# Routing blocks and logits of the first expert layer: table entry moved to the next list, logits in column fourths, unread products at the head

## The chip, the core and the metric

The kernel runs on one core of one Trainium2 chip, as one program with one launch. The metric is the device time of the execution in microseconds (us), as the median of three runs; the profile is one further execution.

## The reference

Attention over 2 batches, 8 heads, 576 positions of 64 numbers, with a mask of blocks of 64 positions, gives 1152 rows of 512. A first expert layer sends each row to one of 8 experts, at most 288 rows to each; a second sends each row to two of 8 experts, by noisy logits.

```python
attn_out = _attn_ref(q, k, v)                      # softmax(q k^T / 8, block mask) v
x = attn_out.transpose(0, 2, 1, 3).reshape(1152, 512)
# first layer: e = argmax(x @ w_gate); kept if fewer than 288 rows came to e before
out[i] = gate_w[i] * (relu(x[i] @ w1[e]) @ w2[e])
# second layer
noisy = x @ w_gate + log1p(exp(x @ w_noise)) * noise
top2 = the two largest of noisy; top2_w = softmax of the two
out[i] = sum over the two e of top2_w * (relu(x[i] @ w1[e]) @ w2[e])
```

## The kernel before

The program has three stages. Attention works through 8 pairs of heads. A planner in the kernel (`Weave`) sets the order of the instructions on every engine when the program is built.

In the first expert layer each expert has a list of instructions, which another planner, `Flow`, puts in order from estimated costs and from a row of numbers in `PAR` (weights on the rest of the path by engine, a seed, due times). For every expert the program holds a small list (up to 128 rows: `one_block`) and a large one (`blocks`, 288 rows); a branch on the number of rows picks one. If an expert has more than 256 rows, a further short list for the last 32 follows the large one. In this execution experts 0 to 4 take the small list, 5, 6 and 7 the large one, and 6 the further one. Below, "list 2" is the list of expert 2. The large weights come from DRAM in units of 512 KB, and ACT and DVE split every unit into a high and a low part (L167, L170) one expert ahead; every product is three passes on TensorE (PE), of high and low parts (L198 to L200), apart from one unit of each expert that is used whole in f32 (L184).

In each list of an expert beside its own products stand three more jobs:

- `splits`: the weights of the next expert.
- `row1` (L1441) and `prep` (L1015 to L1021): POOL gathers the rows of the next expert from the DRAM table `x_d` into `xr` by an indirect DMA; PE transposes them, and ACT and DVE make the high part `xh` and the low part `xl`.
- `post`: the routing of a finished block of 128 rows for the second layer. PE transposes the block (L1243) and ACT copies it (L1247). PE makes the 16 logits of the second layer's gate and noise (`logit`, L1252, four accumulating f32 matmuls that record as eight). A chain of small operations on ACT and DVE (L1256 to L1281) finds the two experts of each row, as a one-hot `M`. PE ranks the rows within their experts (`rank`, L1286 and L1288) and POOL counts them into `cum` (`count`, L1292). DVE works out the two destinations (L1315 to L1325). `slots`, `cells` and `filled` (L1329 to L1340, DVE) spread them into two factors S and C, PE multiplies these (`table`, L1345), and DVE adds the product to the table `T2` (L1349), which tells the second layer which row and weight stands in which place of which expert. On POOL `place` (L1228 to L1233) prepares the row's index and `send` (L1236) scatters the block to `x_d`.

A small list holds one `post` (of the block of the expert before), a large list two (that, and its own first block), the further list one (expert 6's second block), and the first list of the second layer (`KNOWN`) one: 12 in this execution. List 0 has none. In list 7 the rows of the first block of the second layer are already gathered from `x_d` (`rows2`, L1418).

All engines take their instructions in the order of the lists, so a PE instruction that waits holds back all behind it.

Of the kernel before, what the change touches and what calls it, by code (L numbers as in the profile page):

```python
# [12 lines left out]
I32 = mybir.dt.int32  # L13
# [16 lines left out]
PAR = [dict(P=0.05, A=0.2, V=0.3, G=0.2, fit=0.52, late=0.548, dma=2.7, when=5.0, split=0, prep=1.8, post=1.85, last=2.5, seed=8387, noise=0.2),  # L30
       dict(P=0.2, A=0.2, V=0.2, G=0.1, fit=0, late=0.32, dma=2.44, when=10.0, split=6.3, prep=0, post=0.3, last=8.0, seed=5942, noise=0.2),
# [15 lines left out]
def attention_moe_moe2(ctx, tc, q, k, v, wg1, w1a, w2a, cap, wg2, wn2, noise, w1b, w2b, out):  # L47
# [45 lines left out]
    wcat = consts.tile([128, KD, 16], F32, name="wcat")  # L93
# [203 lines left out]
    with ExitStack() as actx:  # L297
# [628 lines left out]

    nc.vector.tensor_scalar(cum, ioe, float(NG), None, op0=OP.mult)
# [5 lines left out]
    class Flow:  # L933
# [4 lines left out]
        def __init__(self, kind=OTHER):  # L938
            self.kind, self.par, self.table = kind, PAR[kind], None
# [279 lines left out]
    def post(F, pd, n=128, deps=(), ranks=None, last=False, early=()):  # L1219
# [5 lines left out]
        def place():  # L1225
            fl = tl["fl"] = small.tile([128, 3], F32, name="fl")
            v = tl["v"] = small.tile([128, 2, 2], F32, name="v")
# [90 lines left out]
        def dest():  # L1318
            d = tl["di"] = small.tile([128, 3, 2], I32, name="di")
# [7 lines left out]
        def slots():  # L1327
            S2 = tl["S2"] = small.tile([128, 2, 128], F32, name="S2", bufs=1)
            nc.vector.tensor_tensor(S2[:n], tl["di"][:n, 1, :, None].to_broadcast([n, 2, 128]),  # L1329
                                    fslot[:n, None, :].to_broadcast([n, 2, 128]), op=OP.is_equal)  # L1330

        def cells():
            g = [n, 2, 8 * NG]
            C1 = tl["C1"] = small.tile([128, 2, 8 * NG], F32, name="C1", bufs=1)
            nc.vector.tensor_tensor(C1[:n], tl["di"][:n, 2, :, None].to_broadcast(g), iog[:n, None, :].to_broadcast(g), op=OP.is_equal)

        def filled():
            g = [n, 2, 2, 8 * NG]
            C2 = tl["C2"] = small.tile([128, 2, 2, 8 * NG], F32, name="C2", bufs=1)
            nc.vector.tensor_tensor(C2[:n], tl["C1"][:n, :, None, :].to_broadcast(g), tl["v"][:n, :, :, None].to_broadcast(g), op=OP.mult)  # L1340

        def table(bank):
            tl["T"] = bank[:, 0:16 * NG]
            for j in range(2):
                nc.tensor.matmul(tl["T"], tl["S2"][:n, j], tl["C2"][:n, j].rearrange("p a g -> p (a g)"), start=(j == 0), stop=(j == 1))  # L1345

        def enter():
            c = T2[:, :, :, 0:NG]
            nc.vector.tensor_tensor(c, tl["T"].rearrange("p (a e g) -> p a e g", a=2, e=8), c, op=OP.add)  # L1349
# [5 lines left out]
        lg = F.add("P", 0.85, logit, [a], take="sm")  # L1355
# [456 lines left out]
```

## Time and profile before

| | before |
|---|---|
| median of 3 runs | 547.79 us (546.66 to 547.98) |
| the profiled execution | 548.82 us, of which the span of the profile 547.2 us |
| PE busy | 514.5 us, 94% |
| DVE, ACT, POOL busy | 69%, 54%, 26% |
| DMA | 99.17 MB, mean 181 GB/s |

The profiled execution is 1.03 us above the median, and its own time 1.62 us above its span. Attention fills the first 138 us or so, the first expert layer goes to about 345 us, the second layer from there to the end. A row of the timeline gives the start and the duration of the instructions merged into it, and in brackets how long the engine had been idle before, and what ended that.

### The profile page before, as it was taken

What the parts mean: (1) busy time and instruction counts of PE and PEld (TensorE: products, weight loads), DVE (VectorE), ACT (ScalarE), POOL (GpSimd) and SP (SyncE); (2) the same over time, 40 slices, a digit from 0 to 9 for tenths busy, and PEclk for the clock granted to TensorE, in tenths of its full rate; (3) what the DMA queues carried; (4) which work ended last, traced back from release to release, by engine and by line L of the source; (5) the groups of instructions that cost most, each with busy time, mean ns of one, the idle gap of its engine ahead of it and who ended that gap; (6) DMA issues with size and microseconds to landing.
All of it is one profiled execution on the core that took longest, in us unless ns stands there. A gap on an engine that the chain in (4) does not pass through costs nothing. (4 is left out here: it accounts for less than half of the span.)

```text
span 547.2 us, 10101 instructions
## 1 busy us (share of the span) xinstructions
PE 514.5 (94%) x3381; PEld 421.4 (77%) x3381; DVE 379.1 (69%) x1008; ACT 294.1 (54%) x580; POOL 143.1 (26%) x225
## 2 busy tenths in 40 slices
PE   3999999999978999999999998999999999999996
PEld 2777777877755876796975976888889797789794
DVE  6889988898748887867575567647657492658441
ACT  5888878882355776653544346335536171726130
POOL 3000000000355344313423224114415051455031
PEclk9999999999999999999999999999999999999999
DMA  6988987501667788754642444528585674285120
GB/s 136 217 196 244 243 224 177 173 2 65 225 213 267 241 264 280 269 181 133 208 123 77 133 151 141 182 90 282 208 299 192 225 264 175 79 311 190 66 67 35
DMA packets 71176, 99.17 MB, mean 181 GB/s; under 512 B 37130, under 2 KB 40586, under 8 KB 71088
## 3 DMA queue, kind: packets, MB, share of 16 engines
q1 hardware_dynamic: 63600, 83.16, 48.4%
q0 software_dynamic: 6432, 14.71, 8.7%
q8 instruction: 39, 0.64, 0.5%
q14 instruction: 49, 0.40, 0.3%
q10 hardware_dynamic: 1056, 0.26, 0.2%
HBM read 87.53 MB, written 12.25 MB: 182 GB/s over the span
## 5 line engine op out<-in xcount | busy, mean ns | idle before, releaser
L170 DVE TENSOR_TENSOR wl<-raw,wh 128x512 fp32r<-128x512 f32 x140 | 91.5, 684 | 12.9 <-ACT wh L167 12.6
L167 ACT ACTIVATE wh<-raw 128x1024 fp32r<-128x1024 f32 x70 | 71.2, 1052 | 20.6 <-PEq L1776 12.5
L170 DVE TENSOR_TENSOR both<-raw,both 128x512 fp32r<-128x512 f32 x100 | 66.0, 684 | 9.0 <-ACT both L167 8.5
L167 ACT ACTIVATE both<-raw 128x1024 fp32r<-128x1024 f32 x50 | 51.4, 1054 | 10.0 <-PEq L1776 8.3
L198 PE MATMUL h<-xh,wh 128*128 128x256 f32 (+1 forms) x184 | 52.8, 287 | 0.5
L199 PE MATMUL h<-xl,wh 128*128 128x256 f32 (+1 forms) x184 | 52.6, 286 | 0.0
L200 PE MATMUL h<-xh,wl 128*128 128x256 f32 (+1 forms) x184 | 52.5, 285 | 0.0
L1018 ACT ACTIVATE xh<-tp 128x512 fp32r<-128x512 f32 (+1 forms) x37 | 18.9, 536 | 56.3 <-PE tp L1015 54.6
L1583 POOL DMA_INDIRECT out_dram<-o,T2i x16 | 18.6, 1164 | 99.7 <-DVE o L1580 97.6
L1021 DVE TENSOR_TENSOR xl<-tp,xh 128x512 fp32r<-128x512 f32 (+1 forms) x37 | 21.8, 609 | 31.1 <-ACT xh L1018 30.9
L1145 ACT ACTIVATE hh<-h 128x512 fp32r<-128x512 f32 (+1 forms) x46 | 24.1, 523 | 34.7 <-PE h L200 29.8
L198 PE MATMUL h<-xh,both 128*128 128x256 f32 (+1 forms) x136 | 39.1, 288 | 2.7 <-DVE hl L1148 1.4
L1148 DVE SCALAR_TENSOR_TENSOR hl<-h,hh 128x512 fp32r<-128x512 f32 (+1 forms) x46 | 27.4, 596 | 18.0 <-ACT hh L1145 16.9
L199 PE MATMUL h<-xl,both 128*128 128x256 f32 (+1 forms) x136 | 39.0, 287 | 0.0
L200 PE MATMUL h<-xh,both 128*128 128x256 f32 (+1 forms) x136 | 38.8, 285 | 0.0
L198 PE MATMUL y<-wh,hh 128*128 128x512 f32 (+1 forms) x94 | 38.3, 408 | 0.0
L200 PE MATMUL y<-wh,hl 128*128 128x512 f32 (+1 forms) x94 | 37.0, 394 | 0.0
L199 PE MATMUL y<-wl,hh 128*128 128x512 f32 (+1 forms) x94 | 37.0, 394 | 0.0
L526 PE MATMUL s<-both 128*128 128x256 f32 (+2 forms) x128 | 33.0, 370 | 4.2 <-ACT both L468 2.5
L550 ACT ACTIVATE pt<-s,negmax 128x128 f32<-128x128 f32 (+3 forms) x64 | 33.4, 526 | 6.3 <-DVE negmax L537 5.1
L198 PEld LDWEIGHTS h<-xh,wh 128*128 128x128 f32 x184 | 34.7, 189 | 1.9 <-issue 1.6
L1437 POOL MEMSET xr<- 128x524 f32 x3 | 1.5, 547 | 132.2 <-DVE T1f L811 132.2
(295 smaller groups left out, 1331.1 us busy)
## 6 DMA issues: line engine op xcount, KB each, us to landing
raw<-in_moe_w_dram SPq DMA_DIRECT2D x120, 512.0 KB, 5.5
wf<-in_moe_w_dram SPq DMA_DIRECT2D x8, 512.0 KB, 4.3
out_dram<-zero SPq DMA_DIRECT2D x3, 768.0 KB, 5.7
both<-both SPq DMA_DIRECT2D x14, 160.0 KB, 2.7
raw<-in_q_dram SPq DMA_DIRECT2D x16, 128.0 KB, 4.3
vn<-in_v_dram SPq DMA_DIRECT2D x16, 128.0 KB, 2.6
both<-both SPq DMA_DIRECT2D x14, 144.0 KB, 2.6
raw<-in_k_dram SPq DMA_DIRECT2D x14, 128.0 KB, 4.6
```

Of the source, the lines that this page charges most:

```text
L167: nc.scalar.activation(h, t, AF.Copy)
L170: (nc.gpsimd if part == 3 else nc.vector).tensor_sub(l[:, c], t[:, c], h[:, c].bitcast(F32))
L198: nc.tensor.matmul(o, sh, mh, start=first, stop=False)
L199: nc.tensor.matmul(o, sh, ml, start=False, stop=False)
L200: nc.tensor.matmul(o, sl, mh, start=False, stop=last)
L526: nc.tensor.matmul(o, w[:, i, h, 128 * t:128 * t + 128], w[:, i + 2, h, 64 * h:64 * h + n], start=(i == 0), stop=(i == 1))
L550: nc.scalar.activation(o, i, AF.Exp, bias=negmax[:, pr, 2 * t + h:2 * t + h + 1], accum_out=ssum[b][:, t, 2 * p + h:2 * p + h + 1])
L1018: nc.scalar.activation(xh[:, :, c0:c0 + n], h["tp"][:, :, :n], AF.Copy)
L1021: nc.vector.tensor_tensor(xl[:, :, c0:c0 + n], h["tp"][:, :, :n], xh[:, :, c0:c0 + n].bitcast(F32), op=OP.subtract)
L1145: nc.scalar.activation(part(hfull[0], g - (KF - 2 * WHOLE) // per) if plain(g) else part(hh, g), of(g), AF.Relu)
L1148: nc.vector.scalar_tensor_tensor(part(hl, g), of(g), 0.0, part(hh, g).bitcast(F32), op0=OP.max, op1=OP.subtract)
L1583: ins = nc.gpsimd.indirect_dma_start(out=out, out_offset=_off(G[key][1][:n, 0:1]), in_=G[key, "o"][:n], in_offset=None, bounds_check=NT - ...
```

## The change

1. `post` no longer enters its block in the table. What it worked out stays in tiles that all blocks share (`cv`, `cdi`), and a new function `enter` does `slots`, `cells`, `filled`, `table` and the addition. Every list from list 1 on begins with an `enter` for the last block that was worked out; a block enters at once (`now`) where another `post` follows in the same list, and in list 7 and `KNOWN`. Since the tiles are shared, the POOL and DVE operations of a `post` that write them wait for the `enter` ahead of it. List 1's `enter` enters nothing (the tiles are zero).
2. The logits: the gate weights, padded to 32 columns, become the stationary side, and the four parts of the sum go to four fourths of the partitions; ACT copies the result out of PSUM, and one more f32 matmul with a 128 x 16 matrix of ones and zeros, `fold`, adds the four.
3. The first row of `PAR` (small lists) and the second (large lists) have other numbers, so that all these lists are planned anew. List 0, the lists of the second layer and attention keep their numbers.
4. At the head of the program PE gets 18 bf16 products of 256 columns ahead of the first transposes and 19 behind those of the first pair; nothing reads them.
5. In list 7 the gather for the second layer waits for the list's `enter`.

```diff
-PAR = [dict(P=0.05, A=0.2, V=0.3, G=0.2, fit=0.52, late=0.548, dma=2.7, when=5.0, split=0, ..., seed=8387, noise=0.2),
+PAR = [dict(P=0.1359, A=0.2225, V=0.3964, G=0.0213, fit=0.0251, late=0.5058, dma=0.3434, when=6.3229, split=0, ..., seed=8016, noise=0.2107),
...
-    wcat = consts.tile([128, KD, 16], F32, name="wcat")
+    wcat = consts.tile([128, KD, 32], F32, name="wcat")
+    fold = consts.tile([128, 16], F32, name="fold")
...
             if b == B:
+                nc.gpsimd.memset(wcat[:, :, 16:32], 0.0)
...
+        def unread(n):
+            for _ in range(n):
+                nc.tensor.matmul(rings["av"][0][:, 0:256], ones, ones[:, None, :].to_broadcast([128, 2, 128]), start=True, stop=True)
...
                 def pe(op):
+                    if not made.get("warm"):
+                        made["warm"] = True
+                        unread(18)
                     for t in range(4):
...
                     nc.tensor.matmul(bank(op, "tp")[:, 0:128], q4.rearrange("p h d -> p (h d)"), eighth, start=True, stop=True)
+                    if pr == 0:
+                        unread(19)
...
+    nc.gpsimd.tensor_tensor(fold, ident[:, 0:16], ident[:, 32:48], op=OP.add)
+    nc.gpsimd.tensor_tensor(fold, fold, ident[:, 64:80], op=OP.add)
+    nc.gpsimd.tensor_tensor(fold, fold, ident[:, 96:112], op=OP.add)
...
+    def enter(F, deps=(), early=(), tail="post"):
...
+        used = [F.table] if F.table else []
+        s2 = F.add("V", 0.33, slots, list(deps[:1]) + used)
+        c = F.add("V", 0.2, cells, list(deps[:1]) + used)
+        c2 = F.add("V", 0.36, filled, [c] + list(deps[1:]) + used)
+        t = F.table = F.add("P", 0.7, table, [s2, c2], take="sm")
+        F.entered = [s2, c2]
+        return F.add("V", 0.22, add, [t] + list(early), frees=t, tail=F.par[tail]), s2
...
         def logit(bank):
-            lg = tl["lg"] = bank[:, 0:16]
+            tl["lb"] = bank
             for kk in range(KD):
-                nc.tensor.matmul(lg[:n], tl["xt"][:, kk, :n], wcat[:, kk, :], start=(kk == 0), stop=(kk == KD - 1))
+                nc.tensor.matmul(bank[32 * kk:32 * kk + 32, 0:n], wcat[:, kk], tl["xt"][:, kk, :n], start=True, stop=True)
+
+        def fourths():
+            lq = tl["lq"] = yT.rearrange("p k n -> p (k n)")[:, 1024:1152]
+            nc.scalar.activation(lq[:, :n], tl["lb"][:, 0:n], AF.Copy)
+
+        def logits():
+            lg = tl["lg"] = tl["lb"][:, 128:144]
+            nc.tensor.matmul(lg[:n], tl["lq"][:, :n], fold, start=True, stop=True)
...
-        f = F.add("G", 0.8, place, deps)
+        f = F.add("G", 0.8, place, list(deps) + F.entered)
...
-        c = V(dest, [c])
+        c = V(dest, [c] + F.entered)
...
-        s2 = V(slots, [c, F.table], 0.33)
...
-        t = F.table = F.add("P", 0.5, table, [s2, c2], take="sm")
-        z = F.add("V", 0.22, enter, [t] + list(early), frees=t, tail=F.par["last" if last else "post"])
+        z = s2 = None
+        tl["read"] = [c, w]
+        if now:
+            z, s2 = enter(F, (c, w), early, "last" if last else "post")
...
-        def beside(F, first):
+        def beside(F, first, more=False):
             done = splits(F, units(e))
-            nxt = post(F, first, last=True)[0] if first is not None else None
+            z = enter(F)[0] if first is not None else None
+            nxt = post(F, first, last=True, now=more or e + 1 == E)[0] if first is not None else None
...
-                d, _ = rows2(F, (0, 0), 0, 0, tis[0])
+                d, _ = rows2(F, (0, 0), 0, 0, tis[0], deps=[z])
...
                 if blk == 0:
-                    post(F, pend[2], deps=r, ranks=nxt)
+                    post(F, pend[2], deps=r, ranks=nxt, now=e + 1 == E)
...
-                _, z, _, tl = post(F, cur)
+                enter(F)
+                _, z, _, tl = post(F, cur, now=e + 1 == E)
```

How the instructions stand now is shown at two places, both in list 2, the small list of expert 2.

The first is PE at the end of the list. `M` is the one-hot of `rank`, C and S the factors of the table, `xr` the rows of the next expert, `hf` and `wf` the part that is used whole. Before:

```order
L1288 MATMUL sm_1719<-M,before 128x8
L1015 MATMUL tp_1716<-ident,xr_1751 128x128 x4
L1080 MATMUL y_1712<-both_107,hl 128x512
L184 MATMUL y_1712<-wf_1746,hf 128x512
L1015 MATMUL tp_1717<-ident,xr_1753 128x32 x4
L184 MATMUL y_1712<-wf_1746,hf 128x512
L1345 MATMUL sm_1718<-C_3511,S_3506 128x144 x2
L1534 UNCONDITIONAL_BRANCH
```

and with the change:

```order
L1313 MATMUL sm_1757<-fold,yT 128x16
L1091 MATMUL y_1751<-both_108,hh 128x512 x2
L1258 MATMUL sm_1758<-C_1775,S_1773 128x144 x2
L1091 MATMUL y_1751<-both_108,hh 128x512 x2
L1094 MATMUL y_1751<-both_108,hl 128x512 x2
L185 MATMUL y_1751<-wf_1795,hf 128x512 x2
L1347 LDWEIGHTS ones
L1347 MATMUL sm_1758<-cum,ones 128x8
L1349 LDWEIGHTS before
L1349 MATMUL sm_1758<-M,before 128x8
```

The table (L1345, now L1258) went from the end into the list; the rank (L1288, now L1349) is now the last work ahead of the branch, and the transposes of the next expert's rows (L1015, now L1029) stand ahead of the logits.

The second is POOL from the start of the same list. Before:

```order
L1228 COPY v<-px_1731 128x2
L1231 ISA
L1231 TENSOR_SCALAR fl<-px_1731 128x1
L1232 TENSOR_SCALAR io<-ioe,fl 128x8
L1233 TENSOR_SCALAR ti<-px_1731,fl 128x1
L1441 DMA xr_1752<-x_d,T_88 128x524
L1441 DMA xr_1751<-x_d,T_88 128x524
L1507 TENSOR_LOAD cnt_91
L1441 DMA xr_1753<-x_d,T_88 32x524
L1236 DMA x_d<-px_1731,ti 1152x524
L1292 TENSOR_TENSOR cum<-cum,M 128x8 x2
L1213 COPY px_1730<-xr_1748 128x9
```

and with the change:

```order
L1479 DMA xr_1800<-x_d,T_89 128x524
L1479 DMA xr_1801<-x_d,T_89 128x524
L1479 DMA xr_1802<-x_d,T_89 32x524
L1546 TENSOR_LOAD cnt_92
L1281 COPY v<-px_1780 128x2
L1284 TENSOR_SCALAR fl<-px_1780 128x1
L1285 TENSOR_SCALAR io<-ioe,fl 128x8
L1286 TENSOR_SCALAR ti<-px_1780,fl 128x1
L1289 DMA x_d<-px_1780,ti 1152x524
L1227 COPY px_1779<-xr_1797 128x9
L1228 COPY px_1779<-T1f 128x3
L1353 TENSOR_TENSOR cum<-cum,M 128x8 x2
```

The gathers (L1441, now L1479) went ahead of `place`, and the count (L1292, now L1353) went behind the copies into `px`, to the end of the list.

## Rows read from the trace of the kernel before

**Rows 1.** The page: the granted clock of PE in 40 slices of the span, in tenths
```profile
PEclk9999999999999999999999999999999999999999
```

**Rows 2.** Busy time by stretch: list 1 (stretch, length, PE, PEld, DVE, ACT, POOL, ...)
```profile
158.58:178.34 19.76, 16.85 (x87) 12.19 (x86) 14.19 (x46) 12.93 (x22) 12.36 (x22) 1.00 0.67 219
```

**Rows 3.** PE's waits, first layer (sum in us, times, longest)
```profile
PE sm L1345 <- DVE C L1340: 3.7, 8, 0.7
PE tp L1015 <- DMA xr<-x_d,T: 3.6, 3, 1.7
```

**Rows 4.** PE's timeline, list 2, and the first row of list 3
```profile
178.34 0.47 PE L198 MATMUL h<-wh,xh 128*128 128x512 f32 x1
...
182.90 0.96 PE L1252 MATMUL sm<-wcat,x2t 128*128 128x16 f32 x8
183.71 0.48 PE L198 MATMUL h<-wh,xh 128*128 128x512 f32 x1
...
184.49 1.07 PE L1077 MATMUL y<-both,hh 128*128 128x512 f32 x4
185.40 0.39 PE L198 MATMUL h<-wh,xh 128*128 128x512 f32 x1
...
194.54 0.76 PE L1345 MATMUL sm<-C,S 128*128 128x144 f32 x4 [0.56 <-DVE C L1340]
195.08 0.47 PE L198 MATMUL h<-both,xh 128*128 128x512 f32 x1
```

**Rows 5.** PE's timeline, attention: products of 32 columns among products of 128
```profile
105.74 0.49 PE L562 MATMUL tp<-ident,pt 128*128 128x128 f32 x3
106.16 0.42 PE L674 MATMUL tp<-xt,wblk 128*32 128x128 f32 x8
106.41 0.27 PE L675 MATMUL tp<-xt,wblk 128*32 128x64 f32 x2
```

**Rows 6.** POOL's timeline, lists 1 and 2
```profile
161.77 0.34 POOL L1228 COPY v<-px 128x2 f32<-128x2 f32 x1
...
174.31 0.47 POOL L1292 TENSOR_TENSOR cum<-cum,M 128x8 bf16<-128x8 bf16 x2 [3.21 <-PE sm L1288]
...
175.66 0.19 POOL L1228 COPY v<-px 128x2 f32<-128x2 f32 x1 [0.62 <-POOL px L1214]
...
177.22 1.21 POOL L1441 DMA_INDIRECT xr<-x_d,T  x1 [0.28 <-issue]
```

**Rows 7.** Gathers, us to landing: list 1's first, list 2's first, second layer's
```profile
xr<-x_d,T POOLq DMA_INDIRECT x1, 6.8
...
xr<-x_d,T POOLq DMA_INDIRECT x1, 5.0
...
g<-x_d,ti POOLq DMA_INDIRECT x2, 3.5
```

**Rows 8.** Groups of PE instructions, first layer: the part used whole
```profile
L184 PE MATMUL y<-wf,hf 128*128 128x512 f32 x44 | 22.5, 604 | 0.0
```

**Rows 9.** PE's timeline, the head of the program
```profile
5.70 1.94 PE L442 MATMUL tp<-ident,raw 128*128 128x128 f32 x8 [5.70 <-DMA raw<-in_k_dram]
7.43 0.64 PE L479 MATMUL tp<-eighth,q 128*128 128x128 f32 x2
...
13.74 1.01 PE L526 MATMUL s<-both 128*128 128x384 f32 x2 [0.68 <-DVE both L876]
...
18.03 0.55 PE L562 MATMUL tp<-ident,pt 128*128 128x128 f32 x3
...
19.88 0.60 PE L442 MATMUL tp<-ident,raw 128*128 128x128 f32 x4
20.25 1.32 PE L531 MATMUL s<-both 128*128 128x288 f32 x8
```

**Rows 10.** ACT's and DVE's timelines, list 2: ends of the chain logits to one-hot
```profile
183.90 0.18 ACT L1256 ACTIVATE a<-sm 128x8 f32<-128x8 f32 x1
...
190.07 0.17 DVE L1281 TENSOR_TENSOR M<-ii,io 128x16 bf16<-128x16 uint32 x1
```

More of the change, by code (lines that the diff above doesn't have):

```diff
@@ L29 @@
 SMALL, LARGE, LARGE_R, SECOND, SECOND_R, KNOWN, OTHER, FIRST = range(8)
-PAR = [dict(P=0.05, A=0.2, V=0.3, G=0.2, fit=0.52, late=0.548, dma=2.7, when=5.0, split=0, prep=1.8, post=1.85, last=2.5, seed=8387, noise=0.2),
-       dict(P=0.2, A=0.2, V=0.2, G=0.1, fit=0, late=0.32, dma=2.44, when=10.0, split=6.3, prep=0, post=0.3, last=8.0, seed=5942, noise=0.2),
+PAR = [dict(P=0.1359, A=0.2225, V=0.3964, G=0.0213, fit=0.0251, late=0.5058, dma=0.3434, when=6.3229, split=0, prep=8, post=3.2145, last=10.5619, seed=8016, noise=0.2107),
+       dict(P=0.4, A=0.0884, V=0.1582, G=0.051, fit=0, late=0.5397, dma=0.8093, when=10.0, split=7.6038, prep=1.8763, post=5.5326, last=0, seed=1201, noise=0.2003),
        dict(P=0.145, A=0.135, V=0.27, G=0.33, fit=0.087, late=0.3, dma=0, when=7.0, split=3.0, prep=0.6, post=2.587, last=13.6, seed=267, noise=0.7),
@@ L938, in __init__ @@
         def __init__(self, kind=OTHER):
-            self.kind, self.par, self.table = kind, PAR[kind], None
+            self.kind, self.par, self.table, self.entered = kind, PAR[kind], None, []
             self.random = random.Random(self.par["seed"])
@@ L1217, in to_pend, with slots, cells, filled @@
         return a, F.add("G", 0.2, cp, [p] + list(deps))
-    def post(F, pd, n=128, deps=(), ranks=None, last=False, early=()):
+    cv = small.tile([128, 2, 2], F32, name="v", bufs=1)
+    cdi = small.tile([128, 3, 2], I32, name="di", bufs=1)
+    cS = small.tile([128, 2, 128], F32, name="S2", bufs=1)
+    cC = [small.tile([128, 2, 8 * NG], F32, name="C1", bufs=1), small.tile([128, 2, 2, 8 * NG], F32, name="C2", bufs=1)]
+    nc.vector.memset(cv, 0.0)
+    nc.vector.memset(cdi, 0)
+    def enter(F, deps=(), early=(), tail="post"):
+        hold = {}
+        def slots():
+            nc.vector.tensor_tensor(cS, cdi[:, 1, :, None].to_broadcast([128, 2, 128]), fslot[:, None, :].to_broadcast([128, 2, 128]), op=OP.is_equal)
+        def cells():
+            g = [128, 2, 8 * NG]
+            nc.vector.tensor_tensor(cC[0], cdi[:, 2, :, None].to_broadcast(g), iog[:, None, :].to_broadcast(g), op=OP.is_equal)
+        def filled():
+            g = [128, 2, 2, 8 * NG]
+            nc.vector.tensor_tensor(cC[1], cC[0][:, :, None, :].to_broadcast(g), cv[:, :, :, None].to_broadcast(g), op=OP.mult)
+        def table(bank):
+            hold["T"] = bank[:, 0:16 * NG]
+            for j in range(2):
+                nc.tensor.matmul(hold["T"], cS[:, j], cC[1][:, j].rearrange("p a g -> p (a g)"), start=(j == 0), stop=(j == 1))
+        def add():
+            c = T2[:, :, :, 0:NG]
+            nc.vector.tensor_tensor(c, hold["T"].rearrange("p (a e g) -> p a e g", a=2, e=8), c, op=OP.add)
+        used = [F.table] if F.table else []
[5 more added lines that the diff above has]
+        return F.add("V", 0.22, add, [t] + list(early), frees=t, tail=F.par[tail]), s2
+    def post(F, pd, n=128, deps=(), ranks=None, last=False, early=(), now=True):
         px, pm, _ = pd
@@ L1226, in place @@
             fl = tl["fl"] = small.tile([128, 3], F32, name="fl")
-            v = tl["v"] = small.tile([128, 2, 2], F32, name="v")
+            v = tl["v"] = cv
             nc.gpsimd.tensor_copy(v[:n, :, 0], pm[:n, 9:10].to_broadcast([n, 2]))
@@ L1318, in dest @@
         def dest():
-            d = tl["di"] = small.tile([128, 3, 2], I32, name="di")
+            d = tl["di"] = cdi
             nc.vector.tensor_copy(d[:n, 0], tl["fb"][:n, 0:2])
@@ L1325, in parts @@
             nc.vector.tensor_single_scalar(d[:n, 2], d[:n, 0], 7, op=OP.arith_shift_right)
[L1327 to L1349, printed above, removed]
         t = F.add("P", 0.43, tr, deps, take="tp", after=0.0 if deps else F.par["late"])
         a = F.add("A", 0.48, cp, [t], frees=t)
-        f = F.add("G", 0.8, place, deps)
+        f = F.add("G", 0.8, place, list(deps) + F.entered)
         sent_ = F.add("G", 1.04, send, [f] + list(deps))
-        lg = F.add("P", 0.85, logit, [a], take="sm")
-        c = F.add("A", 0.1, ex, [lg])
+        lg = F.add("P", 0.45, logit, [a], take="sm")
+        c = F.add("A", 0.25, fourths, [lg])
+        c = F.add("P", 0.25, logits, [c])
+        c = F.add("A", 0.1, ex, [c])
         w = V(plus1, [c])
@@ L1515, in large @@
             begin(F)
-            done, nxt = beside(F, last)
+            done, nxt = beside(F, last, True)
             def fin(y, blk, p, first):
@@ L1527, in large @@
                 F = Flow()
[L1528 to L1529 removed]
+                enter(F)
+                _, z, _, tl = post(F, cur, now=e + 1 == E)
+                product2(F, e, 2, lambda y, blk, p, first: to_pend(F, y, R, lambda: mt[2], 3 * e + 2, cur, p, first, deps=[z, tl["sent"], *tl["read"]]))
                 w = F.add("P", 1.6, lambda b: busy(b, 7), ends, take="h")
```

5 lines of the change are left out of this document (1 added, 4 removed).

## The prediction

> **What bounds the kernel now.** I first read the busy shares and the clock. PE works 94% of the span, and its granted clock stands at the top step of the scale throughout [rows 1], so time is won where PE waits or where its own work shrinks. The change touches only the first expert layer and the head of the program, so the next view is PE's waits in that layer: 3.7 us in eight places for C, the last factor of the table, and 3.6 us in three places for gathered rows [rows 3]. The timeline of PE in list 2 then shows where the first kind sits [rows 4]: the table is the last instruction of the list, PE idles 0.56 us for it, and list 3 starts 0.54 us after it. Nothing could be put into that gap, since PE takes its instructions in order. The last views concern what the new lists lean on: how long the gathers take, and when POOL issues them [rows 6, 7].
>
> **The table's wait.** With the change C is built at the head of the next list from numbers that were ready at the end of the one before, and the table stands in the middle of the list, among products. DVE needs the same three operations as before, so nothing is added there. Seven of the eight waits go. The eighth, the longest with 0.7 us, is that of list 7, where the last block still enters at once behind its rank: it stays. That is 3.7 - 0.7 = 3.0 us. A wait also costs the overlap with the product ahead: the logits begin at 182.90, last 0.96, and the next product begins 0.15 us before their end [rows 4]. Seven times that is 1.05 us. **Gain 4.05 us.**
>
> There are 13 tables in place of 12 (list 1's first is empty, and the entries of list 7 and ahead of it add up to one more). A table takes 0.54 us from its start to the next product [rows 4]. **Loss 0.54 us.**
>
> **The logits.** Before, they held PE for 0.81 us (182.90 to 183.71) [rows 4], eight passes of 0.1. The nearest row for the new form is attention's product by `wblk`: four f32 products of 32 columns into four fourths of the partitions, eight passes in 0.25 us (106.16 to 106.41) [rows 5]. Three transposes stand ahead of it; at the 0.09 us of one such transpose (20.25 less 19.88 for four) [rows 9] the group could have begun at 106.02 and began at 106.16, so a change of shape costs 0.14 us. Then come the two passes of `fold`, 0.2 us at the old price. Together 0.25 + 0.14 + 0.2 = 0.59, a gain of about 0.2 us, 12 times: **gain 2.4 us**. With no cost for the change of shape it is 0.36 us each, 4.3 us; with that cost on both sides of both groups (0.56), nothing.
>
> The Trainium skill, TensorEngine Tiling (Array Packing), section Tiling Modes, says that a change of the tiling mode drains the engine. That speaks against putting narrow products into a stream of wide ones. The trace's 0.14 us agrees with a drain; by the rule with two changes per block the gain would be 0.07 us each, 0.9 us in all.
>
> ACT's copy of the logits is hidden: ACT works 12.93 of list 1's 19.76 us [rows 2]. It lengthens the chain to the rank (below).
>
> **The gathers.** In the new small lists PE reaches the transposes of the next expert's rows after 24 h products, two sets of transposes and no logits. Before, 18 products, the same transposes and the logits took 6.15 us (178.34 to 184.49) [rows 4]; six products at 0.23 us (184.49 to 185.40 for four) more and the logits less give 6.7 us. The rank is now the end of the list, and POOL's count waits for it. From the count to `place` POOL took 1.35 us, and the first gather was issued 0.28 us after the operation ahead of it [rows 6]; without the copies into `px`, now ahead of the count, I take 1.4 us from the start of the list to the gather. It landed after 5.0 us in list 2 and 6.8 in list 1 [rows 7]: PE would wait nothing or 1.5 us. I take 0.3, since the row of list 2 is that of the same place, plus the lost overlap of 0.15, in lists 2 to 4. **Loss 1.35 us** (0 to 4.95).
>
> In list 1 POOL is free for the gather at 161.77, where `place` began [rows 6], so it starts at 162.05, lands between 167.05 and 168.85 and PE, there at 165.3, waits 1.8 to 3.6 us; I take 2.8. Before, the longest of the three waits for gathered rows, 1.7 us, was this one. **Loss 1.1 us** (0.1 to 1.9).
>
> In list 7 the gather for the second layer now waits for the table and stands behind a count. About 1.0 us after the first rank it is issued (count, index, issue), and lands 3.5 us later at the rate of such gathers [rows 7]. PE has nine products at 0.23, a table, `fold` and two passes of the whole part at 22.5/44 = 0.51 us each [rows 8] in between: 3.8 us. It waits 0.75 us, and 0.15 of overlap: **loss 0.9 us** (to 2.4, landing after 5.0).
>
> The three additions that make `fold`, the padding of the weights and two memsets of small tiles are free: POOL and DVE have nothing else to do there before the first gathers. Without that cover they cost some 0.1 us each.
>
> **The head.** The first eight transposes take 1.73 us (5.70 to 7.43), and later four take 0.37 (19.88 to 20.25) [rows 9]: the first run at less than half the pace, though the granted clock reads full. Work from 13.74 to 18.03 is as slow. If the unread products, which fit into PE's idle time up to 5.70 and between the transposes and the scores, bring the faster pace forward, ACT gets its first four transposes 0.5 us earlier, and everything behind it. That is the lower end. The upper one adds half the stretch from 13.74 to 18.03, 2.1 us: 2.6 us. There DVE and ACT work on the same pairs of heads and will not follow in full, so I take **a gain of 1.0 us**, nearer to the lower end.
>
> The Trainium skill, TensorE: Matmul & The Clock Gate, Part 1, says that PE starts at half clock until it has worked for a while. The slow first transposes agree; the row of the granted clock doesn't show it. By that rule alone the stretch would be paid in full, 2.6 us.
>
> **Sum:** 4.05 - 0.54 + 2.4 - 1.35 - 1.1 - 0.9 + 1.0 = 3.56 us off. The profiled execution took 548.82 us, so 545.3; it lies 1.03 us above the median of the runs, so the median comes to 547.79 - 3.56 = **544.2 us**. The logits' upper end alone is 1.9 us away, so this case reaches 1.9 us to either side, from 542.3 to 546.1.
>
> **Rivals.**
>
> - *The gathers land in time* (5.0 us everywhere, 3.5 in list 7 with no wait): 1.35 + 0.9 + 1.0 us better, 540.9 us. For it: list 2's own row. Against: the gathers now compete with the head of the weights' stream.
> - *The head pays in full*, 2.6 us in place of 1.0: 542.6 us. It needs DVE and ACT to follow PE at the faster pace. The Trainium skill's rule on the clock (above) would give this.
> - *Nothing from logits and head*: drains eat the one, and the DMAs of the first pairs set the pace in the other: 2.4 + 1.0 less, 547.6 us, no change.
> - *The gathers land late*, slower than before: at list 1's 6.8 us everywhere, lists 2 to 4 lose 4.95 in place of 1.35, list 1 0.8 more, list 7 1.5 more: 5.9 us, to 550.1. Each us of landing costs about 5 us over five lists, so the gain is gone 0.7 us above the landing that I took (5.6): from 6.3 us on. For it: that row exists. Against: list 2's.
> - *The rank waits at the end of every small list.* From logits to `M` the chain took 6.2 us (183.90 to 190.07) [rows 10]; from `fold` to the rank PE now has four hh and two hl products, the table and four passes of the whole part, 1.4 + 0.54 + 2.0 = 3.9 us. If the chain stays as long, four lists lose 2.3 us each: 9.2 us, 553.4. It decides from a chain of 4.8 us on, where the gain is gone. Against: then, seven splits of weights lay between its steps on DVE, now one.
>
> **Chances.** About 0.3%, 1.6 us, can be told from no change. Forecast 0.51, in time 0.13, head in full 0.08, nothing 0.12, late gathers 0.10, late rank 0.06. The range from 540.8 to 547.6 takes in the forecast's bounds, the two better cases and the one of no change, and leaves out the late ones. Faster (under 546.2): nearly all of the forecast and the better cases, 0.72. No change: the third rival and the milder halves of the late ones, 0.18. Slower: 0.10.
>
> **What would show it.** PE's wait for C should be gone from the ends of lists 1 to 4, and about 0.7 us left in list 7; small lists should take some 16.2 us where list 2 took 16.74. The logits' group and `fold` should take 0.6 us together. Waits of PE for `xr` in lists 2 to 4 above 1 us, or a wait ahead of the rank, would prove me wrong; so would a head in which the first scores start no earlier.

## The result, and the profile after

The changed kernel takes **553.42 us** (median; 552.60 to 558.62), the kernel before, run beside it, 547.67: a ratio of 1.0134, with an interval of [1.0105, 1.0164]. It is 5.7 us slower by the medians (7.3 by the ratio), where I had forecast 544.2 us and a range of 540.8 to 547.6. The profiled execution took 553.43 us with a span of 551.8, 4.6 us longer than the span of before.

First the busy line of PE and the row of its granted clock, from the page of the changed kernel, where [rows 1] showed nines alone:

```profile
PE 520.2 (94%) x3446; PEld 420.9 (76%) x3446; DVE 381.6 (69%) x1014; ACT 297.5 (54%) x592; POOL 146.2 (26%) x229
PEclk9899999999999999999999998999999999999999
```

Two slices have lost clock, one at the head and one behind the first layer. The waits of PE in the first layer (line, what it waited for, us in total, times, longest), to be laid beside [rows 3]:

```profile
PE tp L1029 <- DMA xr<-x_d,T: 6.7, 6, 1.7
PE h L199 <- issue: 1.5, 1, 1.5
PE tp L1029 <- DMA g<-x_d,ti: 1.2, 1, 1.2
PE tp L1296 <- issue: 0.9, 1, 0.9
PE sm L1258 <- DVE C L1253: 0.9, 1, 0.9
PE sm L1498 <- DVE di L1386: 0.9, 1, 0.9
```

The eight waits for C have become one. In their place the waits for gathered rows grew from 3.6 to 6.7 us, a wait for the second layer's rows `g` is new, and so are two stops put down to "issue", time for which no semaphore is seen. The account by lists, from the start of each list's first h product in the two timelines (the last line: what follows the first list of the second layer):

| | before, us | after, us | difference |
|---|---|---|---|
| up to list 0 | 142.23 | 142.81 | +0.58 |
| list 0 | 16.35 | 17.29 | +0.94 |
| list 1 | 19.76 | 16.36 | -3.40 |
| list 2 | 16.74 | 17.11 | +0.37 |
| list 3 | 17.33 | 18.46 | +1.13 |
| list 4 | 16.62 | 17.67 | +1.05 |
| list 5 | 31.32 | 30.84 | -0.48 |
| list 6 and its further list | 41.53 | 42.53 | +1.00 |
| list 7 | 31.41 | 33.61 | +2.20 |
| `KNOWN` | 29.91 | 31.04 | +1.13 |
| the rest | 183.96 | 184.05 | +0.09 |

The lines add up to the 4.6 us between the two spans, not to 5.7, since the profiled execution of the kernel before is one of its longer ones. The first line is no lasting cost of the change: a second execution of the changed kernel (below) began list 0 at 142.25 us.

PE in list 2 of the changed kernel, from its timeline (start, duration, line, operation, in brackets the idle time and its end), which answers to [rows 4]:

```profile
184.14 0.66 PE L1029 MATMUL tp<-ident,xr 128*128 128x128 f32 x4 [1.03 <-DMA xr<-x_d,T]
...
188.15 0.43 PE L1305 MATMUL sm<-x2t,wcat 128*32 128x128 f32 x8
188.50 0.66 PE L1062 MATMUL tp<-ident,yT 128*128 128x128 f32 x4
188.92 0.71 PE L1094 MATMUL y<-both,hl 128*128 128x512 f32 x2
189.46 0.29 PE L1313 MATMUL sm<-fold,yT 128*128 128x16 f32 x2
189.64 0.73 PE L1091 MATMUL y<-both,hh 128*128 128x512 f32 x2
190.21 0.65 PE L1258 MATMUL sm<-C,S 128*128 128x144 f32 x4
...
193.34 0.17 PE L1347 MATMUL sm<-cum,ones 128*128 128x8 bf16 x1
193.57 0.47 PE L199 MATMUL h<-both,xh 128*128 128x512 f32 x1
```

Table, logits and rank are as I priced them: the group of logits holds PE for 0.35 us (188.15 to 188.50) and `fold` for 0.18, against 0.81; the table stands among products, and nothing waits at the end. What is lost is 1.03 us for the rows. POOL shows why (gathers L1479 of lists 2, 3 and 4, and the end of list 7):

```profile
176.45 0.98 POOL L1353 TENSOR_TENSOR cum<-cum,M 128x8 bf16<-128x8 bf16 x2 [6.22 <-DVE both L171]
178.19 1.09 POOL L1479 DMA_INDIRECT xr<-x_d,T  x1 [0.76 <-ACT both L168]
...
195.71 1.25 POOL L1479 DMA_INDIRECT xr<-x_d,T  x1 [1.11 <-ACT both L168]
...
213.97 1.09 POOL L1479 DMA_INDIRECT xr<-x_d,T  x1 [0.90 <-ACT wh L168]
...
327.24 0.48 POOL L1353 TENSOR_TENSOR cum<-cum,M 128x8 bf16<-128x8 bf16 x2 [18.84 <-PE sm L1349]
327.66 0.19 POOL L1447 CAST ti<-T 128x1 int32<-128x1 f32 x1
328.32 1.33 POOL L1456 DMA_INDIRECT g<-x_d,ti  x1 [0.47 <-POOL ti L1447]
```

The first gather of a list is issued 1.7 to 2.1 us after the list's start (176.46, 193.57, 212.03), and PE goes on 6.0, 7.0 and 6.4 us after the issue. What it meets there shows in the windows view (stretch, its length, busy us and count of PE, PEld, DVE, ACT, POOL, clock, DMA share, GB/s), first of before, over the 5.0 us that list 2's gather took there, then of the changed kernel over the three gathers:

```profile
177.20:182.20 5.00, 4.43 (x24) 3.73 (x24) 3.81 (x8) 4.28 (x6) 4.06 (x4) 1.00 0.50 136
```

```profile
178.20:184.20 6.00, 4.97 (x27) 3.79 (x25) 6.00 (x12) 5.21 (x7) 5.10 (x7) 1.00 0.96 319
195.70:202.70 7.00, 4.99 (x24) 3.53 (x22) 6.04 (x11) 5.18 (x7) 5.80 (x8) 1.00 0.97 303
214.00:220.40 6.40, 4.74 (x25) 3.58 (x23) 6.25 (x12) 5.03 (x7) 5.51 (x7) 1.00 0.95 333
```

The DMA engines were half free then and are full now. Three other first gathers fit this: in the kernel before, that of list 1 took 6.8 us [rows 7] at a share of 0.85 and that of list 3 took 5.0 at 0.69; in the changed kernel, that of list 1 was in time after at most 5.0 us at 0.59 (here the first and the last of these):

```profile
165.50:172.30 6.80, 5.18 (x25) 3.98 (x23) 6.61 (x22) 4.46 (x9) 4.68 (x4) 1.00 0.85 260
```

```profile
162.20:167.10 4.90, 4.90 (x26) 3.77 (x25) 4.48 (x8) 4.90 (x8) 4.25 (x4) 1.00 0.59 198
```

No run changes the load alone, so the load as the cause of the longer landing is argued, not shown.

The end of list 7, on PE, and the granted clock behind it (two rows of the same view):

```profile
329.93 1.02 PE L185 MATMUL y<-wf,hf 128*128 128x512 f32 x2
332.12 0.66 PE L1029 MATMUL tp<-ident,g 128*128 128x128 f32 x4 [1.17 <-DMA g<-x_d,ti]
332.61 0.17 PE L1347 MATMUL sm<-cum,ones 128*128 128x8 bf16 x1
332.64 0.19 PE L1349 MATMUL sm<-M,before 128*128 128x8 bf16 x2
332.69 1.10 PE L185 MATMUL y<-wf,hf 128*128 128x512 f32 x2
334.73 0.76 PE L1258 MATMUL sm<-C,S 128*128 128x144 f32 x4 [0.94 <-DVE C L1253]
```

```profile
332.00:336.60 4.60, 2.77 (x16) 1.74 (x17) 2.70 (x15) 2.27 (x3) 2.22 (x7) 1.00 0.17 60
336.60:340.00 3.40, 3.40 (x17) 2.08 (x16) 3.18 (x7) 2.60 (x5) 2.89 (x6) 0.50 0.03 7
```

The rank stands in PE's order behind the transposes of the late rows, so one wait breeds the next: rank, then C, then the table. PE worked 2.77 of these 4.6 us, and the next 3.4 us ran at half the clock, the lower of its two levels, 1.2 GHz.

### The profile page after: what moved, and what is told of

It is laid out like the page before. It is cut to its first block, busy times and chain, and to the rows that moved or that the text cites. A ratio compares the mean times of both kernels' runs of the same rounds, so it can differ in the third digit from the quotient of the medians.

```text
span 551.8 us, 10258 instructions
## 1 busy us (share of the span) xinstructions
PE 520.2 (94%) x3446; PEld 420.9 (76%) x3446; DVE 381.6 (69%) x1014; ACT 297.5 (54%) x592; POOL 146.2 (26%) x229
## 5 line engine op out<-in xcount | busy, mean ns | idle before, releaser
L1032 ACT ACTIVATE xh<-tp 128x512 fp32r<-128x512 f32 (+1 forms) x37 | 18.9, 536 | 52.8 <-PE tp L1029 46.5
L1162 DVE SCALAR_TENSOR_TENSOR hl<-h,hh 128x512 fp32r<-128x512 f32 (+1 forms) x46 | 27.4, 596 | 15.9 <-ACT hh L1159 13.7
```

The source lines that it names most:

```text
L1032: nc.scalar.activation(xh[:, :, c0:c0 + n], h["tp"][:, :, :n], AF.Copy)
L1162: nc.vector.scalar_tensor_tensor(part(hl, g), of(g), 0.0, part(hh, g).bitcast(F32), op0=OP.max, op1=OP.subtract)
```

## The experiments

Every ratio is to the kernel before, run beside the version.

**The changed kernel again**, with no edit.

> The changed kernel once more, for a second profile. Theory A (the loss is in the order of the lists): the same PE waits for gathered rows in lists 2 to 4 (1.0, 0.9, 1.7 us) and at the end of list 7 (1.2 and 0.9 us), within 0.3 us each, and the same half-clock stretches at the head and behind list 7. Theory B (the two stops of 0.95 and 1.47 us that no semaphore explains are instruction transfers that come late by chance of the traffic): those two stops move or change by over 0.5 us, while the waits for rows stay. If both stops come back at the same instruction with the same length, they belong to the layout of the program.

555.31 us, 1.0149 [1.0101, 1.0198]. The waits for rows come back (0.9, 0.4 and 2.0 us in lists 2 to 4; 1.2 and 0.9 in list 7), and so do both stops, at the same two instructions: 0.84 and 1.74 us against 0.95 and 1.47. The stops belong to the program, and theory B is out. The half clock came back behind list 7, but not at the head; instead it stood for 3.4 us each behind the wait of 2.0 us in list 4 and behind the stop of 1.74 us. Theory A holds for the place of the waits, not for the head; two of the waits, in lists 3 and 4, moved by more than its 0.3 us.

**The head alone**, and **the change without it**.

```diff
 before:  + unread(18) ahead of the first transposes, + unread(19) behind the first pair
 changed: - unread(18), - unread(19)
```

> The kernel before with the 18 and 19 unread products at the head alone. My prediction had 1.0 us faster (0.5 to 2.6), so 546.7. Theory now, from the changed kernel's rows: the first scores start 0.5 us earlier, then the granted clock falls to half for some 7 us and the lead turns into a lag of about 0.6 us: 548.3, not to be told from no change by the times, but in the profile the attention's later steps should stand 0.5 to 0.7 us later than before. Rival: the lag in the changed kernel comes from the extra operations on POOL and the longer weight tile, then the head alone shows the lead of 0.5 us all through.

> The changed kernel without the unread products. If they cost 0.6 us as the rows of the head say: 552.8. If they gain what I predicted: 554.4. If the half clock at the head is theirs, no stretch of half clock before 20 us of the span appears (or none is recorded), and the clock's mean rises by 0.006.

The head alone: 548.27 us, 1.0026 [1.0000, 1.0052]. Without it: 554.66 us, 1.0156 [1.0119, 1.0193], no better than with it. The head neither gains nor costs what can be told. Two things stand against it. The first is a transfer, and the second execution of the changed kernel shows it best, since no stretch at half clock follows its products; here are two of its rows, then the same two of the kernel before:

```profile
25.52 1.64 PE L634 MATMUL av<-big,vn 128*64 128x192 f32 x20 [0.35 <-DVE xt L423]
...
29.83 1.45 PE L537 MATMUL s<-both 128*128 128x256 f32 x8 [2.25 <-DMA both<-both]
```

```profile
26.97 1.64 PE L623 MATMUL av<-big,vn 128*64 128x192 f32 x20 [0.35 <-DVE xt L421]
...
29.74 1.45 PE L526 MATMUL s<-both 128*128 128x256 f32 x8 [0.72 <-DMA both<-both]
```

PE's lead of 1.45 us at the product `av` ends at the scores of the second pair of heads: they wait for a DMA that lands at the same time in both. The second is the clock. In the first profile of the changed kernel the first scores start 0.5 us earlier (10.08), but the clock falls to half from 12.4 to 19.2 us, beside PE's waits of 1.00 us (to 10.08) and 1.26 us (to 13.30), and `av` comes 0.34 us late. Nine of the eleven profiles with all 37 products have such a fall at 12 to 13 us; the execution with the lead is one of the other two.

**Gathers two experts ahead**, in the changed kernel and in the kernel before: a third set of tiles for gathered rows, so that a list gathers for the list after the next.

```diff
-    xrs = [[... for i in range(3)] for e in range(2)]
+    xrs = [[... for i in range(3)] for e in range(3)]
-                    d = F.add("G", 1.04, ... row1(e + 1, blk, n)) if e else None
+                    if e + 2 < E:
+                        F.add("G", 1.04, ... row1(e + 2, blk, n))
+                    d = None
```

> The changed kernel with a third set of tiles for gathered rows, so that a list gathers the rows of the expert after the next; PE's order in the small lists stays. Theory A (the rows land too late in lists 2 to 4): PE's waits for xr in lists 2 to 4, 1.03 + 0.92 + 1.67 = 3.6 us, go, with 3 x 0.15 us of lost overlap: 4.1 us less, 549.3. Theory C (DMA traffic is the limit there and the next late transfer, of weights or instructions, takes over): less than half of it, 551.4 or more. The waits in list 0 stay, with up to 1 us more if three gathers more stand in front of it.

> The kernel before with the third set of tiles and gathers two experts ahead. Its one long wait for gathered rows in lists 1 to 4 is that of list 1, 1.7 us; nothing else should move: 1.7 to 1.9 us less, 546.0 against 547.7. If the third set gains here as much as in the changed kernel (5 us), it does something other than taking PE's waits for rows away.

In the changed kernel: **550.04 us, 1.0055 [1.0031, 1.0079]**, 5.3 under the changed kernel beside it. Its profile is that of its fastest run (546.84 us). PE's only wait left for `xr` in the first layer is one in list 0:

```profile
PE h L199 <- issue: 1.6, 2, 1.4
PE tp L1029 <- DMA g<-x_d,ti: 1.2, 1, 1.2
PE sm L1258 <- DVE C L1253: 0.9, 1, 0.9
...
PE tp L1029 <- DMA xr<-x_d,T: 0.6, 1, 0.6
```

Lists 2, 3 and 4 take 15.8, 17.1 and 15.6 us, 4.8 less than in the changed kernel, near the 4.1 of theory A; theory C is out. The lists without a stop or a wait for rows are 1.0 us shorter than before (16.74 and 16.62): the gain that I forecast of table and logits is there. In the kernel before the third set gives nothing: 548.54 us, 1.0038 [0.9980, 1.0096]; list 1 is 2.3 us shorter, list 0, where PE now waits 1.9 us at once, 1.5 us longer.

**Old numbers, and the entry alone.** First the changed kernel with the old two rows of `PAR`; then that without `fold` and unread products.

```diff
-PAR = [dict(P=0.1359, ..., seed=8016, ...), dict(P=0.4, ..., seed=1201, ...),
+PAR = [dict(P=0.05, ..., seed=8387, ...), dict(P=0.2, ..., seed=5942, ...),
```

> The changed kernel with the old numbers for the small and the large lists (entry in the next list, logits in fourths and unread products stay). PE then reaches the next expert's rows only after the logits of the small list, about 2 us later than in the changed kernel. Theory A (the new numbers, which bring the transposes of the gathered rows forward, made the loss): no wait for xr in lists 2 to 4, 3.6 us less than the changed kernel and about 2 us less at the end of list 7, so 549 or less, with the table's waits gone. Theory B (the entry itself costs: rank at the end, gathers behind the count): the waits for xr stay above 2 us in all and the time stays above 551.

> The entry in the next list alone: old numbers, logits in one group as before, no unread products. By my terms 4.05 - 0.54 us for the tables, 0.9 us lost in list 7: 2.6 us less than the kernel before, 545.2. Theory A of the lists (no wait for xr with these numbers): 544 to 546. Theory B (entry costs more than it gains): 548 or more, with waits for xr in lists 2 to 4 or ahead of the rank.

554.04 us, 1.0123 [1.0071, 1.0176], and 556.00 us, 1.0160 [1.0109, 1.0211]. Both of my theories missed: there is no wait for `xr` in lists 2 to 4, and still no gain. The loss sits in one row, here of the entry alone:

```profile
PE tp L1026 <- DMA g<-x_d,ti: 5.6, 1, 5.6
```

The second layer's gather waits for list 7's `enter`, which the old numbers put late, and half the clock follows the 5.6 us for 13.7 us (5.1 and 6.8 us with all of the change). The new numbers had brought that wait down to 1.2 us.

**Nothing left to enter in list 7**: list 6 enters its last blocks at once, and list 7 has no `enter`.

```diff
-            z = enter(F)[0] if first is not None else None
+            z = enter(F)[0] if first is not None and e + 1 < E else None
-    nxt = post(F, first, last=True, now=more or e + 1 == E)[0] ...
+    nxt = post(F, first, last=True, now=more or e + 2 >= E)[0] ...
-                    post(F, pend[2], deps=r, ranks=nxt, now=e + 1 == E)
+                    post(F, pend[2], deps=r, ranks=nxt, now=e + 2 >= E)
```

> The entry alone (old numbers, logits in one group, no unread products), with list 6 entering at once, so that list 7 is word for word that of the kernel before. By my terms for the table, 3.7 - 0.7 - 0.3 (list 6) + 6 x 0.15 - 0.54 = 3.1 us less than the kernel before: 544 to 545. Theory E: close to that, some 10 us under the run of the entry alone (5.6 us of wait and 13.7 us at half clock). Rival: the entry also costs inside the small lists (a wait of 2.2 us for a split of weights showed once), then 547 or more.

> The changed kernel with the old numbers of all lists, and list 6 entering at once. With the old numbers alone PE waited 5.1 us for the second layer's rows at the end of list 7 and ran 6.8 us at half clock behind it (3.4 us lost). Theory E: both go, so 7 to 8.5 us less than the run with the old numbers alone: 545.5 to 547 by its profile, 1 to 2 us under the kernel before. Rival (the new numbers are needed for the entry to pay): no better than 550.

The entry alone falls to 548.20 us, 1.0021 [0.9999, 1.0043], 7.8 us less; all of the change with the old numbers to **545.94 us, 1.0006 [0.9981, 1.0032]**, 8.1 less by the medians (7.6 and 6.4 by the ratios). Theory E is shown for these numbers: the deferred entry of list 7 costs 6 to 8 us with its late gather and the clock behind it. But the entry alone gains nothing even so, as the rival had it (547 or more): its profile has a wait of 2.2 us for a split of weights at the start of list 4, where the kernel before waits 0.5.

> The changed kernel, but list 6 enters its last blocks at once, so that nothing is left to enter in list 7, and list 7 follows the old numbers of the large lists: its end is that of the kernel before. Theory E (what the deferral costs at the end of list 7 is the late gather for the second layer, with the half clock behind the idle PE): PE's waits there fall from 1.2 + 0.9 us to the 0.7 us of the kernel before, no half clock between 325 and 345 us, together 2 to 4 us less than the changed kernel: 550 to 552. The waits for xr in lists 2 to 4 and the two stops that no semaphore explains stay. Rival: the time is in the lists before, and this run stays within 1 us of the changed kernel.

> The same with the third set of tiles for gathered rows (gathers two experts ahead). Both losses undone: 4 to 5 us less than the run with list 7 mended alone, 545 to 547, at or under the kernel before; what then is left of the loss is the two stops of some 0.8 and 1.5 us. If it stays above 549, a third cause of over 2 us is missing from the account.

> The changed kernel with the third set of tiles, and list 7 alone by the old numbers of the large lists, so that its rank and table come ahead of the gathered rows' transposes. Theory D (the rank behind the wait for the rows is what idles PE 1.2 + 0.9 us there, and the idle PE then gets half the clock): the two waits shrink to under 1.0 us in all, no half clock follows between 325 and 345, and the time is 1.2 to 2.5 us under that of the run with the third set alone. Rival: the chain from the last logits to the last table is as long as list 7 lasts, and the wait only moves to the table: less than 0.5 us.

These keep the new numbers and give list 7 the old ones; the last one leaves the deferred entry, with the third set. The first: 556.00 us, 1.0141 [1.0096, 1.0186]. List 7 is mended (31.44 us against 33.61), but list 6, which now enters at once by the new numbers, takes 46.5 us, with the stop of 1.9 us, half the clock behind it, and a wait for C of 1.0 us; the forecast of 550 to 552 missed. So for the new numbers no run mends list 7 and leaves the rest alone.

With the third set: 549.10, 1.0055 [1.0027, 1.0082], above my 547 and just above the 549 from which on a further cause had to be missing; list 6 takes 45.0 us there, against 42.5 with the third set alone.

The last one: 554.57, 1.0114 [1.0054, 1.0174]. Its profile (550.09 us, its fastest run) shows that by the old numbers list 7 waits 4.4 us for `g` with the rank already done, so my theory D was wrong: not the rank behind the wait is the root there, but the gather that needs the entry.

**Both ends mended**: third set, list 6 entering at once, old numbers in lists 6 and 7, new ones in lists 1 to 5; with the 37 products, without them, with 18 and with 8. The last version here has old numbers everywhere, the third set and no products.

> Gathers two experts ahead, list 6 entering at once, lists 6 and 7 by the old numbers of the large lists; small lists and list 5 as changed. Against the run with list 7 alone mended and gathers ahead, list 6 loses its wait for C of 1.0 us and the 0.4 us behind it: 2 us less, 547 and by its profile 545. The two stops in list 3 and at the start of list 6 should stay, since PE's instructions ahead of them are the same. If the rest of the change gains what I predicted of it (tables 3.5, logits 2.4 of which lists 1 to 5 have half), this is 1 to 3 us faster than the kernel before.

> The same without the 37 unread products, so that all later instructions of PE lie 74 places earlier. Theory G (the stops hang on where the instructions lie): the two stops (0.7 in list 3, 1.2 to 1.5 at the start of list 6) vanish or move, as they did in the changed kernel without the products, where a stop of 3.0 us came up behind list 7 instead; 2 us less than the run with the products if none comes up elsewhere. Theory H (they come from the traffic of the lists): both stay, the time stays.

> The lists of the version with gathers two ahead and old numbers in lists 6 and 7, with the first 18 unread products alone, so that PE's later instructions lie 36 places later than without products and 38 earlier than with all 37. Theory G (place in the instruction stream): none of the three stops stands where it stood with 0 or 37 products, or each has another length; if all go, list 6 takes 41.6 us, list 7 31.4 and the list behind it 29.9, 543 in all, faster than the kernel before. Theory H (the place in the lists or the traffic): the stop of 2.7 us behind list 7 or that of 1.4 us at the start of list 6 comes back with its length.

> The same with 8 unread products, 16 places later than with none. Theory G: the stop behind list 7 moves or changes its length by over 0.5 us against the run without products, the time is 543 to 547 by what stops are left. Theory H: 2.7 us behind list 7 again.

> The old numbers everywhere, entry in the next list but at once in list 6, logits in fourths, gathers two ahead, no unread products. Against the same with the products and without the third set (545.9): the rows came in time there in lists 1 to 4, so the third set gains nothing, and the head is hidden behind the transfers of the first pairs: 545 to 547, no change. If the head's products are worth something after all, 1 us more.

| version | median, us | ratio to the kernel before |
|---|---|---|
| both ends mended, 37 products | 546.73 | 1.0001 [0.9979, 1.0024] |
| the same without products | 546.61 | 0.9994 [0.9974, 1.0014] |
| with 18 | 546.99 | 1.0015 [0.9995, 1.0036] |
| with 8 | 552.60 | 1.0119 [1.0090, 1.0147] |
| old numbers, third set, no products | 555.36 | 1.0153 [1.0117, 1.0188] |

So the loss can be undone, and no version beats the kernel before; my forecasts of a gain (1 to 3 us for the first, 2 more for the second) were missed, and so were the 543 to 547 us of the fourth and the 545 to 547 of the last. Where the gain goes shows in the profile without products (span 544.1 us): lists 1 to 4 take 64.8 us where the kernel before takes 70.5, but list 7 and `KNOWN`, with a stop of 2.7 us and half the clock for 3.4 us behind it, 64.6 where it takes 61.3. The stops, in the changed kernel and without products:

```profile
196.97 0.49 PE L1296 MATMUL tp<-ident,px 128*128 128x128 f32 x3 [0.95 <-issue]
...
262.99 0.30 PE L199 MATMUL h<-xh,both 128*128 128x288 f32 x1 [1.47 <-issue]
```

```profile
PE tp L1294 <- issue: 2.7, 1, 2.7
```

With 37 products PE stops in list 3 and at the start of list 6; with 0, 8 or 18 there it does not, but at the first instruction behind list 7, for 2.7 to 3.4 us. List 6 takes 41.6 us then and not 44.8; of these 3.2 us the stop is 1.43 and the half clock behind it most of the rest. With the old numbers in all lists there is no stop over 0.6 us up to the end of list 7, with the products or without. In the stretch from 261.6 to 263.0 us of the changed kernel, which holds the second stop, the DMA view has an instruction transfer:

```profile
q14 instruction: 1, 0.01, 1.4%
```

It lies at 262.6 to 262.8 us, just ahead of PE's next instruction, and two more lie at 196.4 to 196.8 in the stop of list 3. But the version without products has one 2.0 us into its list 6 and no stop there, and a stop of 1.07 us that the version with 18 has in list 0 holds none.

So with these lists the stops hang on what stands ahead in the program, but not as a shift: the stop behind list 7 keeps its place with 0, 8 and 18 products. By the signs I had set, the run without products speaks for theory G, that with 18 for theory H (2.81 us against 2.73), and that with 8 for G by length (3.43) and for H by place; neither theory is shown. All stops begin at or soon behind the branch at the head of a list: at the first instruction behind list 7, 1.0 us into list 6, 2.4 into list 3, 2.8 into list 0. That PE waits there for its instructions is my reading; the trace has no event that ends the stop. The runs with 8 products and with old numbers lost their time elsewhere: list 2 began 3.4 and 3.8 us late, waiting for a unit of weights, with half the clock behind it. Why it was late in these two is open.

**Work in place of the wait**: ten unread products ahead of the transposes of `g` in list 7, eight ahead of its last table.

```diff
+            for _ in range(fill):
+                nc.tensor.matmul(bank[:, 0:256], ones, ..., start=True, stop=True)
```

> The changed kernel with unread products in list 7 alone: ten ahead of the transposes of the second layer's rows, eight ahead of the last table, so that PE works where it waited 1.2 and 0.9 us. Theory F (the half clock behind list 7 comes from the idle PE): no stretch at half clock between 325 and 350 us, list 7 as long as before (33.6 us, within 0.4), the list behind it 29.9 us as in the kernel before and not 31.0; 1.1 to 1.7 us less in all, 552. Rival: the half clock comes all the same (it belongs to the branch or to the traffic), and the time stays or rises by the products' own 2 us.

553.65 us (549.42 to 558.04), 1.0109 [1.0065, 1.0152]. By the ratio that is 1.4 us under the changed kernel's 1.0134, about what theory F asked for, but the intervals overlap and no gain can be told. Its profile, of its fastest run, has no half clock behind list 7, and `KNOWN` takes 29.8 us and not 31.0; list 7 stays at 33.7 us. But the version with gathers two ahead had the same three waits there, unfilled, and no half clock either, so one profile decides nothing here. Theory F fits and isn't shown.

## Why the prediction was wrong

The prices of table and logits held. What failed are the gathers (4.1 us lost in lists 2 to 4 where I had put 1.35), the end of list 7, where I priced a wait of 0.75 us and not what stands behind it (3.33 us with `KNOWN`), the head (no gain for 1.0), and two stops of 2.4 us in all for which I had put nothing. Term by term:

- *The table's wait* (gain 4.05, loss 0.54): right in lists 1 to 6. In list 7 0.94 us stayed, not 0.7, since the rank came late.
- *Logits* (0.59 us for the group and `fold`): 0.53 measured. Two changes of shape at 0.14 us each, as I had worked out beside the drain that the Trainium skill names (TensorEngine Tiling (Array Packing), section Tiling Modes), would have made it 0.74, too much here. My lower bound was summed wrong: with 0.56 us for four changes the sum is 1.01 us against 0.81, a loss of 2.4 us and not nothing.
- *Gathers of lists 2 to 4* (loss 1.35, bounds 0 to 4.95): the mechanism was right, the landing mis-sized. The gather was issued 0.3 to 0.7 us later than my 1.4, and PE went on 6.0 to 7.0 us after it, not 5.6: three waits of 3.6 us, 4.1 with the overlap. I had taken the landing of the row of list 2 [rows 7], of a gather in which the DMA engines were half busy (0.50); now they are full (0.95 to 0.97). The other row of [rows 7], 6.8 us at a share of 0.85, was the nearer one. The rival of late gathers named this at 550.1; its bound for lists 2 to 4, 4.95, holds.
- *Gather of list 1* (loss 1.1): wrong in sign. The gather, at 162.16 as forecast, was in time for PE, which came at 167.14 and not at 165.3: in part luck, since list 1 began 1.52 us later than in the kernel before. List 1 lost its three waits (0.67, 1.68 and 0.57 us) and is 3.40 us shorter. List 0 gave back 0.94, in waits for its rows (3.05 us for 1.94); why these landed later is open.
- *Gather in list 7* (loss 0.9): the wait was 1.17 for 0.75, but the step failed in what I left out: the rank stands behind it in PE's order, so list 7 took 2.20 us more, and the half clock 1.13 us behind it. I priced a wait and not who queues behind it.
- *Head* (gain 1.0): wrong. The first scores do start 0.5 us earlier; the step that failed is "everything behind it". A transfer sets the pace at 29.8 us, and in most profiles the clock falls again before it. The rule of the Trainium skill (TensorE: Matmul & The Clock Gate, Part 1) that PE starts at half clock agrees with the faster first transposes (1.07 us for eight against 1.94); that alone moved no end.
- *Not foreseen*: the two stops, 0.95 and 1.47 us. Their cause stays open.
- *The rank at the end of each small list* (rival, 553.4): the time was near, the mechanism wrong; no small list waited for its rank.

By the account of the lists the change gained 3.9 us in lists 1 and 5 and lost 8.5 elsewhere: 2.55 in lists 2 to 4 net of their own gain, 3.33 behind list 6, 1.00 in list 6 and 1.52 up to list 1.

## What to carry to other kernels

A wait that is taken away must be followed to all who read the result: here the entry at the end of a list was what let the next layer's gather go early, and deferring it cost 6 to 8 us with one set of numbers. Price a transfer by rows in which the DMA engines are as busy as they will be in the new place, and a wait together with what stands behind it in the same engine's order. A faster head is worth only what the first transfer behind it leaves over.

## What the hardware did that I had not expected

- With the new numbers, removing 19 or more of 37 products at the head moved stops of 0.5 to 1.9 us in lists 3 and 6 to one of 2.7 to 3.4 us behind list 7. The Trainium skill, Runtime: NRT & Kernel Launch, section Terms, describes each engine's instruction memory as a FIFO that is refilled in blocks; the transfers in the stops of lists 3 and 6 agree, but one stop holds none, and no run here shows what makes a refill late.
- The granted clock fell to half for 3.4 us or more behind idle stretches in the middle of the program, not in all executions: behind a wait of 2.03 us and a stop of 1.74 us in one, and behind waits of 1.2, 0.9 and 0.8 us that came close together in another.
- A gather beside full DMA engines (0.95 to 0.97) let PE go on after 6.0 to 7.0 us where [rows 7] had 5.0 at a share of 0.50.
